# Routing the first twelve columns of a gated recurrence in one batch instead of eight and four

## The chip, the cores and the metric

The kernel runs on one core of a Trainium2 chip. A core has five engines with queues of their own: TensorE (PE in the profile, its weight loads PEld), VectorE (DVE), ScalarE (ACT), GpSimd (POOL) and SyncE (SP), which here only issues DMAs. The metric is the device time of one execution in microseconds, the median of several runs; it was 335.33 us before the change (three runs, 334.08 to 337.0).

## The reference

Two parts follow each other. The first is a gated linear recurrence over 768 steps for 4 batches and 8 heads of width 48: a complex state is multiplied by a gate of modulus at most 0.999, an outer product of k and v is added to its real part, and q reads it.

```
scale = np.minimum(mag, 0.999) / (mag + 1e-06)
new_re = ar * S_re - ai * S_im ;  new_im = ar * S_im + ai * S_re
S_re, S_im = (new_re + kv, new_im)
y[:, :, t] = np.einsum('bhd,bhde->bhe', q[:, :, t], S_re)
```

The second is a layer of eight experts over the 3072 tokens of width 384 that the first gives. Each token goes to the one expert with the largest logit, where a bias chosen by the token's modality (0 or 1) is added to the logit, and the result is scaled by the softmax weight of that expert.

```
logits = x @ w_gate + modality_bias[modality_id]
e_idx = np.argmax(logits, axis=1)
h = np.maximum(x[mask] @ w1[e], 0.0)
out[mask] = gate_w[mask, None] * (h @ w2[e])
```

## The kernel before

**Units and turns.** The 768 steps are cut into six chunks of 128, so with four batches there are 24 units of 128 tokens. A loop of turns (L450, w from -4 to 24) is a software pipeline over them. In turn w the kernel issues the transposes of unit w+2 (`turned`: PE writes tKT and tQT, ACT copies them to KT and QT), the products inside the chunk of unit w+1 (`inner`: wp, masked by DVE to W, and up, from which DVE makes mid, U and the next state), the output of unit w (`outer`: yp, copied by ACT to yT) and the token rows and logits of unit w-1 (`rows`: xw, whose rows ACT casts into a tile `packed`, and whose logits DVE sums into `lg`, L389). One unit is one column of 128 tokens for the routing.

**Gates.** Two units form a group x. Their gates go through squares, logarithms, tangents, a running sum of angles on PE (`angles`, u, L197) and one of logarithms (`sums`, ls, L243), sines (css) and moduli (pm). Even turns run the logarithm and exponential functions on ACT, odd ones arctangent and sine, each behind a table load (L117). `hats` (L264) multiplies q and k by the waves to QK (L283), which the transposes read. Squares of the last group are made in turn 13.

**Order.** A scheduler lays the instructions of each engine in a fixed queue; an engine runs its queue in order and waits at an instruction until what it needs is there. Some orders are written out by hand: `issue_after` places an instruction behind another, `mark` is such a place, and `ORDERED` (L306) puts the mask of some units behind a hat. All loads go through SP's queue: the gates' parts (L132, L133), q and k (L139, L140), v (L288), the running sums of the chunk before (cb, L207), and the eight-byte modality numbers (`mid`, L576).

**PSUM.** Every product writes a tile that `pair` or `bank` hands out from four slots in rotation (`bufs=4` in `pair`), so a product waits for the reader of the tile that was handed out four earlier.

**Routing.** `make_router` runs at the end of turn 0: constants, the loads of the modality numbers and biases (L574, L576), and from them the bias of every token and expert with five DVE instructions (L592 to L596). `takes` (L396) says when a batch of columns is routed: columns 0 to 7 in turn 8, 8 to 11 in turn 12, 12 to 15 in turn 16, 16 to 19 in turn 20, the rest in turn 24. `Router.take` is a generator that `resume` (L442) carries on. Its first part (L622 to L653) adds the bias, finds the best expert as a one-hot matrix `oneh` and adds up counts `acc`. One turn later its second part has PE count the tokens that go before each token (`rank`, L656 to L663) and DVE makes of it the slot `place` of each row in a table x_rows in DRAM. For the first batch `guess` (L772) then takes the first two experts in use, from a product `cnt` (L705). In later turns the rows are stored, two columns at a time: DVE writes the softmax weight into the rows (L684) and POOL issues an indirect DMA for each column (L685). A batch below column 16 stores from three turns after its `take` on, one pair a turn. The first batch also writes the empty block of x_rows from one row in SBUF (L622).

**Experts.** `Layers` loads the first weights of the two guessed experts into buffers that the gates leave (`w1s` over abs, L882, and `w2s` over css, L891); the second is tied behind the last row store issued by then (L892). Each tile of 256 or 128 rows is loaded (xg, L929), transposed, multiplied by w1 (h_ps, L966) and w2 (y_ps, L981), and scattered (L986). Behind each expert's last token `fill` (L690) copies empty rows from DRAM to DRAM, so that a tile that reaches past the last token reads rows that no output takes; the loads of the first four tiles don't wait for them.

Of the kernel before, what the change touches and what calls it, by code (L numbers as in the profile page):

```python
# [23 lines left out]
def gate_loop(nc, ctx, tc, cpool, ident, q, k, v, a_re, a_im, sel, lg, make_router, make_layers):  # L24
# [345 lines left out]
    def rows(g, b):  # L370
# [9 lines left out]
        m0 = max(c for c in takes.values() if c <= m)  # L380
        if m == m0:
            n = min([c for c in takes.values() if c > m] + [NU]) - m
            packed = un.tile([L, n, Router.W], U32, name=f"packed{n}", bufs=1 if n == 8 else 2)
            nc.gpsimd.iota(packed[:, 0:n, Router.W - 1].rearrange("p (g b) -> p g b", b=B), pattern=[[L, n // B], [S, B]], base=g * L, channel_multiplier=1)
            box["packed"] = packed
        packed = box["packed"]
# [9 lines left out]
    takes = {7: 0, 11: 8, EARLY - 1: 12, 19: EARLY, NU - 1: 20}  # L396
# [53 lines left out]
    for w in range(-4, NU + 1):  # L450
# [12 lines left out]
        else:  # L463
# [5 lines left out]
            if w > 3:  # L469
                hats(n + 4)  # L470
# [10 lines left out]
        unit(inner, n + 1)  # L481
        resume(lambda w0, n: n > 1 and w0 < EARLY and w >= w0 + 3)
# [19 lines left out]
        resume(lambda w0, n: n == 1 or w0 >= EARLY and w >= w0 + 2)  # L502
        if w - 1 in takes:
            open_.append([rt.take(takes[w - 1], w, late, box["packed"], lambda n: dense(box["full"][:, 0], n)), w, 1])
            next(open_[-1][0])
# [9 lines left out]
class Router:  # L515
# [20 lines left out]
    def __init__(self, nc, ctx, tc, keep, ps, bank, lg, x_rows, moe_modality_id, moe_modality_bias, N, Dt, E, B, G):  # L536
# [35 lines left out]
        mb = rc.tile([TP, nM, E], F32, name="mb")  # L572
        mid = rc.tile([TP, NT, 2], I32, name="mid")
        nc.sync.dma_start(out=mb.rearrange("p m e -> p (m e)"), in_=moe_modality_bias.rearrange("m e -> (m e)")[None, :].broadcast_to([TP, nM * E]))  # L574
        for b in range(B):
            nc.sync.dma_start(out=mid.rearrange("p (g b) w -> p b g w", b=B)[:, b], in_=moe_modality_id[b * G * TP:(b + 1) * G * TP].bitcast(I32).rearrange("(g p w) -> p g w", p=TP, w=2))  # L576
# [11 lines left out]

        bias = self.bias = rc.tile([TP, NT, E], F32, name="bias")
# [7 lines left out]
        self.acc = None  # L597
# [9 lines left out]
    def take(self, m0, m1, late, packed, dense):  # L607
# [4 lines left out]
        M = 8  # L612

        def t(name, shape, dt=F32):
            full = rp.tile([TP, M] + shape, dt, name=name)
            return full[:, 0:n]
# [60 lines left out]
        for i in range(n):  # L677
            if i % 2 == 0:
                if i:
# [3 lines left out]
                with self.tc.issue_after(self.mark.ins):  # L683
                    nc.vector.reciprocal(packed[:, i:i + 2, self.W - 2].bitcast(F32), sums[0][:, i:i + 2])  # L684
# [417 lines left out]
```

## Time and profile before

| | us |
|---|---|
| median of three runs | 335.33 |
| the profiled execution | 336.66 |
| its span, from the first to the last instruction | 335.1 |
| PE busy, 4955 matmuls | 296.6 |
| DVE busy | 243.4 |
| ACT busy | 240.5 |
| POOL busy | 65.7 |

The span is what the trace covers; the time of the execution holds 1.6 us more around it. Rows of the trace begin with the start in us from the span's begin and the duration in us; at the end, in brackets, stands how long the engine was idle before, and what ended it. A view by windows gives for each stretch its length, then the busy time of PE, PEld, DVE, ACT and POOL with the number of instructions, the clock that was granted to TensorE as a share of full speed, the share of DMA engines busy and the GB/s. The view of one source line gives for each kind of instruction the count, the shortest, median and longest duration in ns, and the first and last start. The recurrence takes about the first 250 us; the expert layers take the rest.

### The profile page before, as it was taken

How to read it: one execution, taken by the hardware profiler on the slowest of the kernel's cores; microseconds unless marked ns; L12 is line 12 of the kernel's file. 1: busy time of each engine (PE TensorE's matmuls, PEld its weight loads, DVE VectorE, ACT ScalarE, POOL GpSimd, SP SyncE). 2: the span in 40 equal slices, each digit the busy share in tenths (PEclk: the TensorE clock that was granted, in tenths of full speed). 3: DMA queues.
4: the chain of work that ended last, by engine and by line, in shares of the span. 5: the costliest groups of instructions: out<-in, count | busy, mean ns of one | idle time of the engine just before them, and what ended most of it. 6: DMA issues, size and time to landing. Idle time of an engine off the chain costs nothing.

```text
span 335.1 us, 11585 instructions
## 1 busy us (share of the span) xinstructions
PE 296.6 (89%) x4955; PEld 228.7 (68%) x4955; DVE 243.4 (73%) x464; ACT 240.5 (72%) x290; POOL 65.7 (20%) x92
## 2 busy tenths in 40 slices
PE   1685999899989999997999999999997699999991
PEld 0342576577787868684786879888895377777770
DVE  2759699999999989968599969972458433646430
ACT  3888799999998999796797978535235356454541
POOL 8000000000000000002134224034034425242423
PEclk9999799999999999997899999999999789999997
DMA  7968898799776767798379972114912722333211
GB/s 146 208 129 162 148 200 141 124 179 180 164 131 153 134 146 41 129 220 153 83 146 161 177 165 51 25 50 64 223 54 84 226 94 97 104 110 107 103 67 56
DMA packets 155282, 43.04 MB, mean 128 GB/s; under 512 B 145602, under 2 KB 151494, under 8 KB 155096
## 3 DMA queue, kind: packets, MB, share of 16 engines
q1 hardware_dynamic: 149592, 31.98, 49.9%
q0 software_dynamic: 5632, 10.25, 11.4%
q8 instruction: 41, 0.67, 0.8%
q14 instruction: 17, 0.14, 0.1%
HBM read 38.00 MB, written 9.15 MB: 141 GB/s over the span
## 4 chain that ended last, share of the span: by engine, by line
PE 47%; ACT 22%; SPq 10%; DVE 6%; DMA 5%; issue 5%; POOL 1%; another core or an unknown queue 1%; POOLq 0%; DVEq 0%; ACTq 0%
PE h_ps L966 9%; PE y_ps L981 9%; PE up L336 5%; ACT sq L120 5%; PE xw L377 4%; ACT L117 4%; ACT css L120 3%; PE yp L366 3%; ACT pm L120 3%; PE ls L243 3%; PE wp L326 3%; PE u L197 3%; DMA qk<-in_k_dram 2%; PE yp L360 2%; SPq L132 2%
## 5 line engine op out<-in xcount | busy, mean ns | idle before, releaser
L685 POOL DMA_INDIRECT x_rows<-packed,place x24 | 29.6, 1233 | 66.2 <-DVE packed L684 17.6
L283 DVE TENSOR_TENSOR QK<-css,qkp 128x1536 f32<-128x1536 f32 x24 | 42.0, 1750 | 0.2
L981 PE MATMUL y_ps<-w2t,hT 128*128 128x384 bf16 x200 | 37.3, 341 | 3.9 <-ACT hT L969 3.9
L336 PE MATMUL up<-V,QK 64*96 64x48 f32 x704 | 37.8, 247 | 1.7 <-DVE lg L389 1.6
L336 PEld LDWEIGHTS up<-V,QK 64*96 64x96 f32 x704 | 34.7, 161 | 3.8 <-DVE lg L389 2.4
L966 PE MATMUL h_ps<-xgT,w1t 128*128 128x256 bf16 (+1 forms) x312 | 35.3, 270 | 0.0
L986 POOL DMA_INDIRECT out_dram<-y_sb,xg x25 | 24.9, 996 | 43.5 <-ACT y_sb L984 39.5
L966 PEld LDWEIGHTS <-w1t 128*128 128x128 bf16 x312 | 29.8, 99 | 5.0 <-issue 0.3
L117 ACT ACT_TABLE_LOAD x25 | 32.1, 1283 | 1.4 <-PEq L1086 0.9
L308 ACT COPY KT<-tKT 96x1024 f32<-96x1024 f32 x24 | 24.1, 1006 | 10.2 <-PE tKT L307 10.1
L981 PEld LDWEIGHTS <-hT 128*128 128x128 bf16 x200 | 19.4, 101 | 17.5 <-ACT hT L969 4.5
L882 POOL DMA_DIRECT2D abs<-in_moe_w_dram x2 | 1.8, 898 | 149.3 <-ACT sq L120 149.3
L984 ACT ACTIVATE y_sb<-y_ps,xg 128x384 f32<-128x384 f32 x25 | 13.2, 578 | 23.2 <-PE y_ps L981 18.8
L326 PEld LDWEIGHTS wp<-QT,KT 96*64 96x64 f32 x768 | 24.3, 138 | 8.1 <-ACT yT L367 1.9
L367 ACT COPY yT<-yp 128x512 f32<-128x512 f32 x24 | 14.0, 584 | 21.3 <-PE yp L366 21.1
L326 PE MATMUL wp<-QT,KT 96*64 96x64 f32 x768 | 27.6, 225 | 1.6 <-ACT yT L367 1.3
L377 PE MATMUL xw<-sel,yT 64*128 64x56 f32 x384 | 27.4, 277 | 1.0 <-ACT QT L308 0.6
L197 PE MATMUL u<-tan,turn 128*128 128x384 f32 x48 | 22.4, 550 | 5.0 <-ACT yT L367 2.4
L377 PEld LDWEIGHTS xw<-sel,yT 64*128 64x128 f32 x384 | 24.1, 187 | 3.1 <-ACT QT L308 0.7
L308 ACT COPY QT<-tQT 96x1024 f32<-96x1024 f32 x24 | 24.3, 1012 | 0.3 <-PE tQT L307 0.3
L120 ACT ACTIVATE sq<-sq 128x1536 f32<-128x1536 f32 (+1 forms) x20 | 23.3, 1165 | 1.4 <-DVE sq L151 1.3
L969 ACT ACTIVATE hT<-h_ps 128x1024 bf16<-128x1024 f32 (+1 forms) x17 | 16.9, 999 | 8.9 <-PE h_ps L966 3.0
(198 smaller groups left out, 594.7 us busy)
## 6 DMA issues: line engine op xcount, KB each, us to landing
abs<-in_a_re_dram SPq DMA_DIRECT2D x24, 192.0 KB
abs<-in_a_im_dram SPq DMA_DIRECT2D x24, 192.0 KB
qk<-in_q_dram SPq DMA_DIRECT2D x24, 192.0 KB
qk<-in_k_dram SPq DMA_DIRECT2D x24, 192.0 KB
V<-in_v_dram SPq DMA_DIRECT2D x24, 192.0 KB
cb<-f_scr SPq DMA_DIRECT2D x10, 384.0 KB
xg<-x_rows SPq DMA_DIRECT2D x12, 194.0 KB
x_rows<-x_rows SPq DMA_DIRECT2D x8, 194.0 KB
```

Source lines behind the costliest of these rows:

```text
L117: then(nc.scalar.preload_act_table_set(name))
L120: then(nc.scalar.activation(*args, **kw))
L197: nc.tensor.matmul(us[:, i], turn[:], tan[:, i], start=True, stop=False)
L283: box["hat"] = nc.vector.tensor_tensor(QK[:].rearrange("p a h c d -> p a (h c d)"), wave, twice, Alu.mult)
L308: nc.scalar.copy(to[:], tp)
L326: nc.tensor.matmul(wp[rows_, h, :], KT[:, s, h], QT[:, s, h], start=True, stop=True)
L336: ins = nc.tensor.matmul(up[:, s, h], flat[rows_, h * C:(h + 1) * C], V[rows_, h, 0:D], start=True, stop=True)
L377: ins = nc.tensor.matmul(xw[:, u, j], yT[at_u, j], sel[at_u, j], start=True, stop=True)
L685: put = self.put = nc.gpsimd.indirect_dma_start(out=self.x_rows, out_offset=bass.IndirectOffsetOnAxis(ap=place[:, i:i + 1], axis=0), in_=p ...
L966: nc.tensor.matmul(h_ps[:, f // nf, f % nf, :], w1t[:, k, ff * 128:(ff + 1) * 128], xgT[:, k, :], start=(k == 0), stop=(k == KD - 1))
L981: nc.tensor.matmul(y_both[:, s], self.hT[:, f, s * 128:(s + 1) * 128], w2t[:, f, :], start=(f == 0), stop=(f == NF - 1))
L986: sc = self.sc = nc.gpsimd.indirect_dma_start(out=self.out, out_offset=bass.IndirectOffsetOnAxis(ap=xg[:, Dt // 2 + 1:], axis=0), in_=y_sb ...
```

## The change

Four edits are made.

- Columns 0 to 11 are routed as one batch in turn 12; the batch of eight in turn 8 is gone, and with it the one of four. `guess` and the write of the empty block move with it. The rows of these columns are still kept in a tile of eight and tiles of four. Their stores begin in turn 15, with columns 8 to 11, two pairs in that turn and one in each later one, up to turn 19.
- The loads of the modality numbers and biases move from turn 0 to turn 8, and the five DVE instructions from turn 0 to turn 12, behind the mask of that turn.
- In turn 15 the hat of unit 19 is issued behind the mask instead of ahead of it.
- Each fill copies 128 empty rows instead of 256.

```
-            if w > 3:
+            if w > 3 and w != 15:
                 hats(n + 4)
...
+        if w == 15:
+            with tc.issue_after(box["masked"].ins):
+                hats(n + 4)
...
-    takes = {7: 0, 11: 8, EARLY - 1: 12, 19: EARLY, NU - 1: 20}
+    takes = {11: 0, EARLY - 1: 12, 19: EARLY, NU - 1: 20}
...
+        if w == 8:
+            rt.load_bias()
+        if w == 12:
+            with tc.issue_after(box["masked"].ins):
+                rt.make_bias()
-        resume(lambda w0, n: n == 1 or w0 >= EARLY and w >= w0 + 2)
+        resume(lambda w0, n: n == 1 or w0 >= EARLY and w >= w0 + 2 or w0 < EARLY and w == w0 + 3)
...
-        M = 8
+        M = 12 if n == 12 else 4
...
-        for i in range(n):
-            if i % 2 == 0:
-                if i:
+        for k, i in enumerate(list(range(8, n)) + list(range(min(n, 8)))):
+            rows, c = packed(m0 + i)
+            if k % 2 == 0:
+                if k:
...
-            self.put_row(nc.sync.dma_start(out=self.x_rows[bass.ds(n0, 2 * self.TP), :], in_=self.blank), True)
+            self.put_row(nc.sync.dma_start(out=self.x_rows[bass.ds(n0, self.TP), :], in_=self.blank[0:self.TP]), True)
```

`load_bias` and `make_bias` hold the lines that were in the router's constructor:

```
    def load_bias(self):
...
        nc.sync.dma_start(out=mb.rearrange("p m e -> p (m e)"), in_=moe_modality_bias.rearrange("m e -> (m e)")[None, :].broadcast_to([TP, nM * E]))
        for b in range(B):
            nc.sync.dma_start(out=mid.rearrange("p (g b) w -> p b g w", b=B)[:, b], in_=moe_modality_id[b * G * TP:(b + 1) * G * TP].bitcast(I32).rearrange("(g p w) -> p g w", p=TP, w=2))
    def make_bias(self):
...
        for m in range(nM):
            is_m = rc.tile([TP, NT], F32, name="is_m")
            nc.vector.tensor_scalar(is_m[:], mid[:, :, 0], float(m), None, Alu.is_equal)
```

More of the change, by code (lines that the diff above doesn't have):

```diff
@@ L571, in __init__ @@
         nc.gpsimd.memset(self.fast[:, self.NE + self.NR:self.NE + self.NR + 1], 1.0)
[L572 to L576, printed above, removed]
         self.io = rc.tile([TP, 32], F32, name="io")
@@ L611, in take @@
         last = m1 == len(self.tile_of)
-        M = 8
+        M = 12 if n == 12 else 4
         def t(name, shape, dt=F32):
-            full = rp.tile([TP, M] + shape, dt, name=name)
+            full = rp.tile([TP, M] + shape, dt, name=name + str(M), bufs=1 if M == 12 else 2)
             return full[:, 0:n]
```

30 lines of the change are left out of this document (21 added, 9 removed).

## The prediction

> **What bounds the kernel now.** I began with the page's span and engine shares, and then cut the span into pairs of loop turns.
>
> ```profile
> span 335.1 us, 11585 instructions
> PE 296.6 (89%) x4955; PEld 228.7 (68%) x4955; DVE 243.4 (73%) x464; ACT 240.5 (72%) x290; POOL 65.7 (20%) x92
> ```
> ```profile
> core 0: us, PE busy (x) PEld busy (x) DVE busy (x) ACT busy (x) POOL busy (x), PEclk, DMA share, GB/s
> 85.77:102.63 16.86, 15.72 (x352) 12.86 (x348) 16.14 (x24) 16.36 (x19) 0.00 (x0) 1.00 0.74 144
> 137.49:157.63 20.14, 16.66 (x362) 13.87 (x363) 17.30 (x40) 16.58 (x20) 1.01 (x1) 0.91 0.89 167
> 157.63:179.39 21.76, 20.69 (x392) 15.75 (x391) 16.88 (x35) 16.54 (x19) 7.35 (x6) 0.92 0.66 123
> 195.44:211.78 16.34, 16.28 (x384) 13.85 (x385) 14.38 (x31) 11.52 (x14) 4.89 (x4) 1.00 0.42 95
> ```
>
> The shares mislead: ACT's 72% is a mean of two halves. From 85 us on, ACT has 16.4 us of work in a pair of turns whatever the pair takes, and fills a pair of 16.9. DVE is close behind. The pairs that begin at 137 and 157 are 3 to 5 us longer with no more ACT work in them, and of the pairs shown they alone have a granted clock of PE under 1.00. By 195 PE is the bound. So the question is what stops ACT between 137 and 179. ACT's timeline says it; yT is copied once per turn, and these are the odd turns 7 to 17 with the longest idle times between them:
>
> ```profile
> 118.97 0.59 ACT L367 COPY yT<-yp 128x512 f32<-128x512 f32 x1
> ...
> 135.84 0.59 ACT L367 COPY yT<-yp 128x512 f32<-128x512 f32 x1
> ...
> 138.46 1.01 ACT L308 COPY KT<-tKT 96x1024 f32<-96x1024 f32 x1 [1.65 <-PE tKT L307]
> ...
> 152.13 1.49 ACT L120 ACTIVATE sq<-abs 128x1536 f32<-128x1536 f32 x1
> ...
> 154.93 0.59 ACT L367 COPY yT<-yp 128x512 f32<-128x512 f32 x1
> ...
> 160.53 1.01 ACT L308 COPY KT<-tKT 96x1024 f32<-96x1024 f32 x1 [4.63 <-PE tKT L307]
> ...
> 177.25 0.59 ACT L367 COPY yT<-yp 128x512 f32<-128x512 f32 x1
> ...
> 194.44 0.59 ACT L367 COPY yT<-yp 128x512 f32<-128x512 f32 x1
> ...
> 210.12 0.59 ACT L367 COPY yT<-yp 128x512 f32<-128x512 f32 x1 [2.25 <-PE yp L366]
> ```
>
> The periods are 16.87 (turns 7 to 9), 19.09 (9 to 11), 22.32 (11 to 13), 17.19 (13 to 15) and 15.68 (15 to 17). I take 17.0 as undisturbed: 16.87, and 16.86 for the pair from 85.77. The excess is then **2.1 us** in turns 9 to 11 and **5.3 us** in turns 11 to 13. PE's rows give the cause:
>
> ```profile
> 135.12 0.91 PE L197 MATMUL u<-tan,turn 128*128 128x384 f32 x2
> ...
> 136.84 0.19 PE L659 MATMUL rank<-oneh,tri 128*128 128x64 bf16 x1
> 136.87 0.32 PE L663 MATMUL rank<-oneh,ones 128*128 128x56 bf16 x7
> ```
> ```profile
> 155.57 1.65 PE L197 MATMUL u<-tan,turn 128*128 128x384 f32 x2 [2.43 <-ACT yT L367]
> 161.59 0.91 PE L243 MATMUL ls<-lm,half 128*128 128x384 f32 x2 [0.58 <-ACT KT L308]
> ```
> ```profile
> 150.78:154.19 3.41, 2.36 (x69) 2.08 (x60) 3.41 (x5) 3.39 (x4) 0.25 (x1) 1.00 0.73 107
> 154.19:157.60 3.41, 2.03 (x4) 1.24 (x5) 3.41 (x5) 1.70 (x3) 0.76 (x1) 0.50 0.96 185
> 157.60:161.02 3.42, 3.41 (x35) 1.95 (x34) 2.09 (x5) 0.49 (x1) 2.05 (x2) 0.50 1.09 206
> 62.03:65.45 3.42, 2.29 (x20) 1.72 (x21) 3.42 (x6) 3.39 (x6) 0.00 (x0) 1.00 0.83 69
> ```
>
> All PSUM tiles share four rotating slots. In turn 9 the routing of the first eight columns takes two of them (rank and cnt). From then until the next routing every product reuses the slot of another reader than before: in turn 11, u (155.57) stands 2.43 us until yT is copied, where u of turn 9 follows xw at once. Then the granted clock is 0.50 for 6.8 us, and tKT reaches ACT 4.63 us late.
>
> **The change part by part.** I sum against the profiled execution (336.66 us, span 335.1) and shift the result to the median.
>
> *Turns 9 to 13: the early routing goes.* No rank and cnt in turn 9, so in the built order u of turn 11 waits for DVE as in other turns. What is late next is ACT itself. Both periods fall to 17.0: **-2.1 and -5.3**. Bounds: nothing, if something else holds u; -8.2 for both at the 16.6 us of ACT's busy time.
>
> *The biases.* Five DVE instructions move from turn 1 to turn 12, and their five loads from turn 0 to turn 8.
>
> ```profile
> L592 DVE TENSOR_SCALAR is_m<-mid x2: 164/164/165, 68.7 to 70.0; 128x24 f32<-128x24 int32 x2
> L594 DVE TENSOR_TENSOR bias<-is_m,mb x1: 349/349/349, 69.6 to 69.6; 128x192 f32<-128x192 f32 x1
> 60.50 2.41 SPq L576 DMA_DIRECT2D mid<-in_moe_modality_id_dram  x4
> ```
>
> Their durations add to 2 x 0.16 + 3 x 0.35 = 1.4 us; overlapping their neighbours they hold DVE about 1.0. Taking them from turn 1, where ACT is the bound, and SP's 2.4 us with them, I put at **-0.2** (0 to -1.4). On SP they now stand in turn 8 ahead of V and qk, whose users come two turns later: 0, up to +2.4 if that cover goes. The write of the empty block, in turn 8 so far, moves to turn 12, a like place with fewer loads: 0 (-1 to +2).
>
> *Turn 13: twelve columns routed at once.* In the built order, turn 13's DVE work is W, l, mid, mx, U, sh, state, cand, the sum of squares, best, oneh. Compare turn 9:
>
> ```profile
> 133.60 0.68 DVE L327 TENSOR_TENSOR W<-wp,mask 128x512 f32<-128x512 f32 x1
> ...
> 135.38 0.22 DVE L635 TENSOR_TENSOR oneh<-cand,best 128x64 bf16<-128x64 f32 x1
> ...
> 136.16 0.55 DVE L348 TENSOR_TENSOR state<-U,mt 96x384 f32<-96x384 f32 x1
> 136.62 0.95 DVE L151 TENSOR_TENSOR sq<-sq 128x768 f32<-128x768 f32 x1
> ```
>
> From the start of W to the end of oneh were 2.0 us there. Each overlaps the next by some 0.09, so I count W at 0.6, three like state at 0.46, the sum of squares at 0.87 and six small ones at 0.18 (an estimate for 96 elements, from 0.22 less the overlap for 64): 3.9. The biases delay W by 1.0, less 0.3 for l and mx, which stood ahead of it. So oneh is 2.6 us later than in turn 9, where it ended at 135.60, 1.24 us ahead of the first rank matmul at 136.84. PE, in order, stands **about 1.4 us** at rank (0.5 to 2.6); queued behind it are cnt, both transposes, ls and wp, and ACT's KT copy waits for them. The period 13 to 15 is then 19.09 (turns 9 to 11 with the same slots) + 1.4 + 0.2 for four more rank matmuls - 1.4 for the square of 152.13 that turn 15 no longer has = 19.3, against 17.19 now: **+2.1** (0 to +4). That the second batch of four no longer runs here is in this comparison.
>
> *Turns 15 to 17.* The shifted slots now hold here, and u of turn 15 waits for yT in the built order.
>
> ```profile
> 194.52 0.91 PE L197 MATMUL u<-tan,turn 128*128 128x384 f32 x2
> ```
>
> Without the square, yT is copied by 195.03, so u stands 0.5 us and ls perhaps 0.6 as at 161.59: **+1.1** (0 to +2.4, the hole of turn 11). The qkp and QK of unit 19, moved behind W in turn 15, feed a turn whose bound is PE: 0.
>
> *POOL and the weights.* The first twelve columns' rows now leave in turns 15 to 19, so up to two more indirect stores stand ahead of the first w2 load.
>
> ```profile
> 229.24 0.97 POOL L685 DMA_INDIRECT x_rows<-packed,place  x1 [0.30 <-issue]
> 230.20 0.95 POOL L891 DMA_DIRECT2D css<-in_moe_w_dram  x1
> 231.00:243.40 12.40, 12.40 (x300) 11.23 (x300) 5.36 (x20) 4.21 (x7) 1.22 (x3) 1.00 1.08 178
> 246.65 0.94 DVE L920 COPY w2t<-css 128x3072 bf16 x1
> ```
>
> They delay it by 2 x 1.28 = 2.6 us. Its traffic ends at 243.4 and its last user begins at 246.65, so 3.2 us cover it: 0 (to +2 where the stores take twice as long). Without that cover DVE would stand at w2t with the next lg queued behind it, and PE with it.
>
> *Empty rows.* Eight fills of 194 KB become 97 KB.
>
> ```profile
> 255.85 9.89 SPq L699 DMA_DIRECT2D x_rows<-x_rows  x8
> 267.12 0.16 DVE L806 TENSOR_SCALAR column<-smine 1x19 int32<-1x19 f32 x1
> ```
>
> The next loads on SP's queue need the columns that DVE makes at 267.12, when the fills have been issued (255.85 + 9.89 = 265.74): 0 (-3 if their traffic is what slows PE's second tile).
>
> Sum: -2.1 - 5.3 - 0.2 + 2.1 + 1.1 = **-4.4 us**. 336.66 becomes 332.3; the median of 335.33 becomes **331.0**.
>
> **A rule against the row.** The trace has the clock at 0.50 behind a gap of 2.43 us, and at 1.00 in the window from 62.03 with 1.1 us of PE idle. The Trainium skill ("TensorE: Matmul & The Clock Gate", section "HAM oscillation — how this bites in real kernels") says that only idle gaps of PE over about 3.4 us throttle it. By that rule the gap of turn 11 would have cost no clock, and removing it less; this trace disagrees, and the sum goes by the trace.
>
> **The rivals.** (B) *The stall moves whole.* PE's wait at rank in turn 13 is the mechanism. If PE idles as in the window from 150.78 (1.05 us of 3.41) with that window's light work, the clock halves there too, and u of turn 15 finds the full hole. The moved stretch then costs what the old one did, 2.1 + 5.3, less the 0.2 of excess that turns 13 to 15 have now, plus 0.7 for W and the 1.4 at rank: 336.66 - 7.6 + 9.3 = 338.4, or 337.0 by the median, slower than before. It decides from 1.05 us of idle; my 1.4 is above that, but 62.03 shows 1.1 without a drop, which is why this is not the forecast. (C) *The tail gains.* PE's second expert tile around 260 runs beside the fills; if they slow it, half the bytes give another 3 us: 328. Against it: no row shows an engine waiting for them. (D) *It does not do what it says*: u of turn 11 is held by another late copy, and only turn 9's share goes, which turn 13 returns: 335.
>
> **How the numbers follow.** Forecast 0.48, B 0.30, C 0.10, D 0.12. One per cent, 3.4 us, is about what a measurement of this kernel tells from no change. The forecast's own range is 328.5 to 333.5; two thirds of it is more than 1% faster. With C nearly whole, faster is 0.44. Slower takes a third of B, and its bounds with two late terms, the w2 load and the empty block's write: 0.18. The rest, 0.38, is within 1%. The range runs from C's lower part, 326, past B to 338.5.
>
> **What would show it.** Right: no idle of 2 us at u of turn 11, a granted clock of 1.00 through turns 11 and 12, two periods near 17; rank of turn 13 waiting for DVE oneh or acc; a period near 19 for turns 13 to 15. Wrong: a clock of 0.5 around turns 13 to 16; ACT still idle for over 1 us at KT in turn 12; idle of DVE ahead of w2t.

## The result, and the profile after

The changed kernel takes **354.78 us** (median of five runs, 349.28 to 359.86) against 334.62 us before: a ratio of 1.051, with a 95% interval of 1.037 to 1.066. Forecast were 331.0 us and a range up to 338.5. The profiled execution took 354.78 us, its span is 353.2 us. Ratios, here and below, compare only the executions near the fastest of each kernel (here 349.28 and 354.51 us, with a granted clock of 0.93 and 0.92 over the span, where the profiled execution before had 0.97), so they are not quotients of the medians.

The head of the page after, with the granted clock of PE in 40 slices of 8.8 us:

```profile
span 353.2 us, 11567 instructions
PE 316.6 (90%) x4954; PEld 246.2 (70%) x4954; DVE 243.3 (69%) x451; ACT 240.2 (68%) x289; POOL 67.0 (19%) x92
PEclk9989899999999999999999855975569899999998
```

The same line of the page before:

```profile
PEclk9999799999999999997899999999999789999997
```

DVE and ACT work as long as before (243.3 and 240.2 us); PE is busy 20 us longer with one matmul less. The early dip (7 in the 19th slice before) is gone; in its place the 23rd to 30th slices, 194 to 265 us, lie between 5 and 9. Cut into pairs of loop turns (turns 9 to 11, 11 to 13, 13 to 15, 15 to 17, then 17 to 19 and 19 to 22), the columns as in the prediction:

```profile
138.68:156.18 17.50, 17.01 (x392) 14.14 (x394) 16.14 (x23) 16.49 (x20) 0.00 (x0) 1.00 0.88 162
156.18:174.14 17.96, 16.66 (x348) 13.06 (x342) 17.85 (x34) 16.33 (x19) 0.00 (x0) 1.00 0.59 97
174.14:193.55 19.41, 17.68 (x405) 14.74 (x407) 15.82 (x39) 15.23 (x20) 1.80 (x2) 1.00 0.76 132
193.55:217.40 23.85, 22.21 (x350) 19.67 (x348) 14.26 (x33) 11.64 (x14) 11.45 (x9) 0.64 0.48 104
217.40:236.83 19.43, 18.52 (x371) 15.47 (x368) 12.11 (x45) 7.48 (x12) 9.29 (x6) 0.85 0.16 43
236.83:266.68 29.85, 29.85 (x472) 26.95 (x470) 9.40 (x27) 7.02 (x11) 3.94 (x5) 0.58 0.50 88
```

The first two rows are what was hoped for: 20.14 and 21.76 us have become 17.50 and 17.96, at a clock of 1.00. From 193.55 on the clock is 0.64, 0.85 and 0.58. The yT copies of the odd turns 9 to 17 on ACT's timeline say the same without DVE's part in it:

```profile
137.68 0.59 ACT L367 COPY yT<-yp 128x512 f32<-128x512 f32 x1
...
155.18 0.59 ACT L367 COPY yT<-yp 128x512 f32<-128x512 f32 x1
...
172.05 0.59 ACT L367 COPY yT<-yp 128x512 f32<-128x512 f32 x1
...
190.32 0.59 ACT L367 COPY yT<-yp 128x512 f32<-128x512 f32 x1
...
215.00 0.59 ACT L367 COPY yT<-yp 128x512 f32<-128x512 f32 x1 [6.51 <-PE yp L366]
```

The periods are 17.50, 16.87, 18.27 and 24.68, in place of 19.09, 22.32, 17.19 and 15.68. From these copies the whole difference of 18.1 us adds up:

| stretch | before, us | after, us | difference |
|---|---|---|---|
| start of the span to yT of turn 9 | 135.84 | 137.68 | +1.8 |
| yT of turn 9 to turn 15 | 58.60 | 52.64 | -6.0 |
| yT of turn 15 to the last yT | 53.04 | 77.33 | +24.3 |
| last yT to the end | 87.6 | 85.6 | -2.0 |

(The last yT copies are at 247.48 and 267.65. The first row is nothing of the change: its 1.8 us are there at the first yT copy, and in a later profile of the same kernel that copy is 1.3 us earlier.)

Where the 24.3 us come from is in the windows between the switches of the clock. Every drop in these traces that ends inside the span lasts a whole number of times 3.41 us (3.41, 6.83, 10.24 and so on, up to 44.4); "a window" below is one such time.

```profile
196.87:200.29 3.42, 2.44 (x53) 2.11 (x49) 0.02 (x1) 3.39 (x5) 2.22 (x3) 1.00 1.07 250
200.29:220.77 20.48, 20.48 (x302) 18.44 (x302) 14.10 (x51) 7.91 (x10) 7.21 (x5) 0.50 0.30 69
220.77:234.42 13.65, 13.12 (x311) 11.43 (x310) 9.05 (x20) 4.56 (x7) 8.69 (x6) 1.00 0.20 52
234.42:261.73 27.31, 26.92 (x363) 23.94 (x362) 5.55 (x22) 6.95 (x11) 4.53 (x6) 0.50 0.53 94
```

Half clock for 20.48 + 27.31 = 47.8 us; PE is the bound here and busy all the time, so half of it, 23.9 us, is lost. In the kernel before no drop lasted over 6.83 us. What stands ahead of the first drop, on PE's timeline in turn 16:

```profile
197.42 1.04 PE L336 MATMUL up<-V,QK 64*96 64x48 f32 x19
198.75 0.37 PE L336 MATMUL up<-V,QK 64*96 64x48 f32 x4 [0.28 <-issue]
199.46 0.40 PE L336 MATMUL up<-V,QK 64*96 64x48 f32 x5 [0.34 <-issue]
200.22 0.57 PE L336 MATMUL up<-V,QK 64*96 64x48 f32 x4 [0.35 <-issue]
```

and on POOL's at the same time:

```profile
194.54 1.09 POOL L707 DMA_INDIRECT x_rows<-packed,place  x1 [11.91 <-DMA qk<-in_q_dram]
195.93 1.21 POOL L707 DMA_INDIRECT x_rows<-packed,place  x1 [0.31 <-issue]
197.44 0.97 POOL L707 DMA_INDIRECT x_rows<-packed,place  x1 [0.30 <-issue]
198.72 0.97 POOL L707 DMA_INDIRECT x_rows<-packed,place  x1 [0.30 <-issue]
```

POOL issues the four row stores of turn 15 one right behind the other. PE, which waits for no semaphore, goes on in bursts of four or five matmuls, one burst each 0.71 to 0.76 us. PE's instructions come by DMA in blocks of 16 KB, and none of these blocks was on its way between 197.1 and 204.4, so these bursts are not a wait for one. Its signals come late as well: W on DVE, whose input wp was done at 197.5, starts at 200.27.

```profile
200.27 0.69 DVE L327 TENSOR_TENSOR W<-wp,mask 128x512 f32<-128x512 f32 x1 [3.42 <-remote]
```

The same picture, stores at 231.49, 232.76 and 234.04 and bursts up to 235.7, stands ahead of the drop at 234.42.

### The profile page after: what moved, and what is told of

Its sections match the earlier page's. It is cut to its first block, busy times and chain, and to the rows that moved or that the text cites. A ratio compares the mean times of both kernels' runs of the same rounds, so it can differ in the third digit from the quotient of the medians.

```text
span 353.2 us, 11567 instructions
## 1 busy us (share of the span) xinstructions
PE 316.6 (90%) x4954; PEld 246.2 (70%) x4954; DVE 243.3 (69%) x451; ACT 240.2 (68%) x289; POOL 67.0 (19%) x92
## 4 chain that ended last, share of the span: by engine, by line
PE 33%; issue 19%; ACT 18%; DVE 14%; POOL 6%; SPq 4%; DMA 3%; POOLq 1%; DVEq 0%; ACTq 0%
PE up L336 6%; POOL out_dram L1008 5%; PE xw L377 5%; PE yp L366 5%; ACT sq L120 4%; PE wp L326 3%; PE u L197 3%; ACT L117 3%; ACT css L120 3%; PE yp L360 3%; PE ls L243 2%; PE tKT L307 2%; PE tQT L307 2%; ACT pm L120 2%; DMA qk<-in_k_dram 2%
## 5 line engine op out<-in xcount | busy, mean ns | idle before, releaser
L336 PE MATMUL up<-V,QK 64*96 64x48 f32 x704 | 42.0, 258 | 2.5 <-DVE lg L389 1.5
L707 POOL DMA_INDIRECT x_rows<-packed,place x24 | 30.8, 1283 | 61.8 <-DVE w2t L942 24.0
L336 PEld LDWEIGHTS up<-V,QK 64*96 64x96 f32 x704 | 38.7, 172 | 5.0 <-DVE lg L389 2.2
L1003 PE MATMUL y_ps<-w2t,hT 128*128 128x384 bf16 x200 | 36.5, 336 | 1.7 <-issue 1.0
L326 PEld LDWEIGHTS wp<-QT,KT 96*64 96x64 f32 x768 | 27.4, 152 | 8.3 <-ACT yT L367 2.3
L326 PE MATMUL wp<-QT,KT 96*64 96x64 f32 x768 | 30.9, 240 | 1.7 <-ACT yT L367 1.7
L377 PE MATMUL xw<-sel,yT 64*128 64x56 f32 x384 | 30.6, 302 | 1.1 <-ACT QT L308 0.6
L377 PEld LDWEIGHTS xw<-sel,yT 64*128 64x128 f32 x384 | 26.9, 210 | 3.7 <-issue 0.9
L197 PE MATMUL u<-tan,turn 128*128 128x384 f32 x48 | 22.3, 549 | 3.1 <-ACT tan L120 2.1
L327 DVE TENSOR_TENSOR W<-wp,mask 128x512 f32<-128x512 f32 x24 | 16.4, 685 | 11.2 <-PE wp L326 7.7
```

The source lines that it names most:

```text
L197: nc.tensor.matmul(us[:, i], turn[:], tan[:, i], start=True, stop=False)
L326: nc.tensor.matmul(wp[rows_, h, :], KT[:, s, h], QT[:, s, h], start=True, stop=True)
L336: ins = nc.tensor.matmul(up[:, s, h], flat[rows_, h * C:(h + 1) * C], V[rows_, h, 0:D], start=True, stop=True)
L377: ins = nc.tensor.matmul(xw[:, u, j], yT[at_u, j], sel[at_u, j], start=True, stop=True)
L707: put = self.put = nc.gpsimd.indirect_dma_start(out=self.x_rows, out_offset=bass.IndirectOffsetOnAxis(ap=place[:, i:i + 1], axis=0), in_=r ...
L1003: nc.tensor.matmul(y_both[:, s], self.hT[:, f, s * 128:(s + 1) * 128], w2t[:, f, :], start=(f == 0), stop=(f == NF - 1))
```

## The experiments

Theories held at the start: **S**, a run of row stores on POOL holds PE up, and the clock falls for it; **L**, it is the two w1 loads in a row (180.61 and 181.84) that crowd the queues, and the stores only happen to be there; **H**, at half clock only products that fill the array bring the clock back. **E**, on the write of the empty block, was formed later. The kernel before, run beside each group, took about 337 us in some groups and about 329 us in others, so each kernel is compared with its own group alone. The chip does not tell the two kinds apart: the one numbered 7 in the record gave 329 us in two groups and 337 us in a third. What does is open.

### Stores in a row (before: 336.8 us)

One pair of stores a turn:

```
-        resume(lambda w0, n: n == 1 or w0 >= EARLY and w >= w0 + 2 or w0 < EARLY and w == w0 + 3)
+        resume(lambda w0, n: n == 1 or w0 >= EARLY and w >= w0 + 2)
```

> The changed kernel, with the rows of columns 0 to 11 stored one pair a turn (turns 15 to 20) instead of two pairs in turn 15. In the changed kernel PE issues in bursts with pauses of 0.57 us at 198.2 to 200.2 and again at 232.3 to 235.7, while POOL issues four and three indirect stores one right after the other, and the granted clock falls to 0.50 at 200.29 and 234.42. Theory S (a run of four stores holds PE up, and the clock falls for it): no pauses and a clock of 1.00 through turns 15 to 17; the stores of two batches still meet in turns 18 and 19, so the second drop may stay; 338 to 347 us. Theory L (both w1 loads in a row crowd the queues and hold PE up; the stores only happen to be there): the first drop stays, 350 to 358 us.

Measured 349.4 us, 1.040 (1.029 to 1.051). The first drop is gone, the second stays. In its profile the clock is 1.00 up to 225.04:

```profile
190.00:225.04 35.04, 32.03 (x717) 26.98 (x718) 28.72 (x78) 18.01 (x24) 17.76 (x12) 1.00 0.46 98
225.04:252.35 27.31, 26.16 (x346) 23.02 (x347) 5.62 (x22) 7.05 (x11) 7.26 (x9) 0.50 0.56 103
```

and POOL has the stores that precede it, four at 221.82, 223.10, 224.38 and 225.66:

```profile
221.82 0.98 POOL L707 DMA_INDIRECT x_rows<-packed,place  x1 [0.30 <-DVE mid L341]
...
225.66 0.98 POOL L707 DMA_INDIRECT x_rows<-packed,place  x1 [0.30 <-issue]
```

PE's bursts stand from 222.4 to 227.0. Turn 18 and turn 19 released their pairs while POOL was held by an earlier store, so they left together. This speaks for S; the median lies above what S named, since the second drop took 27.3 us.

The second w1 load moved behind the stores of turn 17:

```
-        for s in range(2):
+        for s in range(1):
             nc.gpsimd.dma_start(out=self.w1s[:, s:s + 1], in_=self.w1[:, bass.ds(self.guessed(s), 1)])
...
+        if turn == 17:
+            got = self.nc.gpsimd.dma_start(out=self.w1s[:, 1:2], in_=self.w1[:, bass.ds(self.guessed(1), 1)])
+            self.tc.add_manual_dep(got.ins, self.rt.put.ins.name, ...)
```

> The changed kernel with the second w1 load behind the stores of turn 17 instead of right behind the first at 181.8 us; the stores are as they were. Theory L (the two loads together crowd the queues, and PE's pauses at 198 come of it): no pauses in turn 15, first drop gone, 340 to 348 us. Theory S (the run of four stores): pauses and drop stay, within 1% of the changed kernel's 354.8 us, 350 to 359 us.

353.8 us (347.5 to 359.5): nothing won, as S had it. The profile is divided: no bursts behind the stores of turn 15 (197.15 to 201.45), though one pause of 1.39 us, up to 199.54, and no long drop there, as L had it; the bursts stand behind the stores of turn 17 (212.9 to 214.8), and the drop that lasted is the second, 13.65 us from 234.52, where no load of w1 is near. So the loads bear on which run of stores does harm, but L explains neither the second drop nor the time.

The kernel before, with the stores of columns 8 to 11 all in turn 15 and those of 12 to 15 all in turn 18:

```
-        resume(lambda w0, n: n == 1 or w0 >= EARLY and w >= w0 + 2)
+        resume(lambda w0, n: n == 1 or w0 >= EARLY and w >= w0 + 2 or w0 == 12 and w == 15)
+        resume(lambda w0, n: w0 == 16 and n > 1 and w == 18)
```

> The kernel before, with the two pairs of stores of columns 8 to 11 both in turn 15 and those of columns 12 to 15 both in turn 18; nothing else is changed. Theory S: PE pauses behind these stores and the clock falls in or after turn 15 or 18, where few full-array products follow; 339 to 350 us. Theory L: 332 to 337 us, as the kernel before, and a clock of 1.00 there.

351.6 us (343.4 to 367.7) against 336.8, a little over what S named. Its profile has a drop of 13.65 us from 235.11, right behind four stores (229.56 to 234.14). It also has one of 10.24 us from 98.58, ahead of any row store: PE was busy for 2.47 us of the window before that, with waits of 0.42 us for yT and 0.72 us for lg. The yT copies of turns 5 and 6 are 14.28 us apart there, 9.58 before, so 4.7 us of this profile's loss are not the stores'. The kernel before with the write of the empty block in turn 5 (further down) has the same two waits at the same times, but its windows begin 0.66 us later and hold 2.99 and 2.69 us of busy PE, and there the clock stays at 1.00. Where the windows happen to begin may have a part in what one execution shows.

The same kernel in another group, with the changed kernel itself, before at 337.8:

> The kernel before with the stores of columns 8 to 11 all in turn 15 and those of 12 to 15 all in turn 18, again. Theory S: slower than the kernel before by 7 us and more where PE pauses behind four stores, and within 1% of it where it doesn't.

> The changed kernel itself, beside the others. In the last three runs no PE pauses stand behind a run of four stores, and the kernel before was at 329.4 us in place of 336.8 (another chip). Theory S: the loss hangs on these pauses. Where they show in the trace, 348 to 360 us with the clock at 0.50 for 40 us behind turn 15; where they don't, the clock stays at 1.00 there and the change is 1 to 5 us faster than the kernel before of the same call, as the sum of the prediction had it (-4.4). If the loss came back without pauses, S would fall.

The kernel with the burst: 361.3 us (355.3 to 364.0). The changed kernel: 351.5 us, 1.035 (1.028 to 1.042), with drops of 17.06 us from 201.49 and 27.30 from 232.21. So two lines that only put stores together turn the kernel before into one as slow as the changed one. In the profile of the second run, which has no drop at 98 us, four stores leave between 224.40 and 228.98, PE's bursts stand from 227.1 to 230.7, and then:

```profile
223.27:230.09 6.82, 5.65 (x115) 4.82 (x111) 3.04 (x7) 0.70 (x1) 4.77 (x5) 1.00 0.14 46
230.09:274.47 44.38, 43.96 (x565) 39.27 (x565) 12.69 (x41) 10.73 (x19) 5.88 (x7) 0.50 0.36 66
```

The DMA share of 0.14 in the first row says that full queues aren't needed for it. The four stores of turn 15 in these two runs left no long drop behind them.

Six memsets of 128x256 on POOL between one pair and the next, for columns 0 to 15:

```
+                if k % 2:
...
+                    for _ in range(6):
+                        self.space = nc.gpsimd.memset(self.scratch[:], 0.0)
...
```

> The changed kernel with six small POOL memsets (2 to 2.5 us) between one pair of stores and the next for columns 0 to 15; the turns in which the pairs are released are as in the changed kernel, two pairs in turn 15 among them. Theory S in its narrow form (it is the stores one right behind the other, not their number in a turn): no bursts of PE 0.57 us apart, no long drop, within 2% of the kernel before (331 to 343 us where that is 337). Rival (the number of stores in these turns, or the bytes): pauses and drops as in the changed kernel, 347 to 358 us.

345.5 us, 1.026 (1.013 to 1.038), before at 337.5. Neither side: the first long drop is gone, but with pairs 3.6 us apart PE still shows two or three pauses behind a pair (from 228.5 and from 232.9 on, up to 0.38 us each), and the clock falls at 236.08 for 13.65 us. So stores need not be four in a row to go with pauses.

### What brings the clock back

Four full-array products ahead of the transposes of units 18, 20 and 22 (before at 336.8):

```
-    FILLED = {2: 10, 3: 5, 4: 5, 5: 5, 15: 4}
+    FILLED = {2: 10, 3: 5, 4: 5, 5: 5, 15: 4, 18: 4, 20: 4, 22: 4}
```

> The changed kernel with four full-array bf16 products of 512 columns (warm 0.22 us, at half clock 0.43 us each) ahead of the transposes of units 18, 20 and 22 (turns 16, 18 and 20). In the changed kernel the clock stays at 0.50 for 20.5 and 27.3 us although PE is 100% busy in those windows with products of 64 or 96 rows, and returns behind windows that hold full-array products (ls at 217, rank at 258). Theory H (at half clock only full-array products bring the clock back): each fill ends a drop within two windows of 3.4 us; half clock after 190 us is about 15 us in place of 48, worth some 16 us less 2.6 us for the fills: 338 to 345 us. Rival (the clock returns when the cause of the stall is over): half clock as long as before, 354 to 360 us.

342.4 us, 1.019 (1.009 to 1.030): in the range. But not the way it was expected. The first drop, at 201.09, ended after 6.83 us with no fill in it. The fill of unit 22 stood at 230.01, among the pauses, and no second drop came:

```profile
227.91:231.33 3.42, 3.10 (x35) 1.98 (x31) 0.00 (x0) 0.00 (x0) 2.56 (x3) 1.00 0.23 77
```

The same fills on a quarter of the array (64 rows and 64 columns), before at 337.8:

```
+                for _ in range(4 if u in (18, 20, 22) else 0):
+                    nc.tensor.matmul(full[0:64]..., halfb[0:64, 0:64], halfb[0:64, None, :].broadcast_to([64, 4, L]), start=True, stop=True)
```

> The changed kernel with the fills on 64 rows and 64 columns, again, since without pauses there was no drop that they could end. Where pauses and a drop show: theory H has the clock stay at 0.50 for 20 us and more, 350 to 360 us; the rival (busy time counts) 338 to 346 us. Where none show: 1% at most from the kernel before.

353.8 us (345.5 to 368.3). The fill of unit 22 stands at 234.32, and the drop comes and stays:

```profile
231.43:234.84 3.41, 2.75 (x39) 2.11 (x34) 0.00 (x0) 0.00 (x0) 2.80 (x3) 1.00 0.28 92
234.84:262.15 27.31, 27.31 (x365) 23.94 (x364) 5.56 (x22) 7.05 (x11) 3.97 (x6) 0.50 0.52 92
```

PE is busy in all 27.31 us, at half clock. Counted over the 20 profiles of this case, between 60 and 300 us there are 146 windows at half clock: of the 69 without a 128x128 product 5 were the last of their drop, of the 58 in which such products took 1.5 us or more of PE's time 48 were. Those five are the fullest of the 69, if fullness is the sum of rows x columns x streamed columns over the products that start in a window. That fits H in a softer form, the used share of the array counts; this is a count after the fact, and what exactly is measured, the runs don't say.

An earlier run of the same kernel fell into a group with before at 329.4:

> The changed kernel with fills at the same places and of the same length as those that brought it to 342 us (four bf16 products of 512 columns ahead of the transposes of units 18, 20 and 22), but on 64 rows and 64 columns of the array in place of 128 and 128. Theory H (what counts for the clock is the part of the array that works): the clock stays at 0.50 for 20 us and more behind turn 15 or 18, as without fills; 352 to 360 us. Rival (what counts is PE's busy time, or that a product is long): the clock returns as with the full fills; 338 to 346 us.

327.9 us, 0.999 (0.995 to 1.003). Here four stores in a row, from 195.22 to 200.95, had no effect at all:

```profile
195.22 1.09 POOL L709 DMA_INDIRECT x_rows<-packed,place  x1 [11.91 <-DMA qk<-in_q_dram]
...
199.41 1.54 POOL L709 DMA_INDIRECT x_rows<-packed,place  x1 [0.31 <-issue]
```
```profile
195.15:201.97 6.82, 6.82 (x156) 5.51 (x154) 5.77 (x9) 6.44 (x8) 4.81 (x4) 1.00 0.95 199
```

PE has no pause and no drop up to the end of the recurrence. So S holds in the groups where the kernel before takes 337 us, and not in those where it takes 329. The changed kernel itself was not run in one of the latter; this kernel is the changed one with three fills of 1.05 us, and its median stands 1.5 us under the kernel before, which the interval does not tell from none. Without the 3.15 us of fills it might stand 3 to 5 us under, near the forecast gain; that is an estimate, and no run shows it. The kernel before itself differs between the two kinds of groups by 1.4 us up to the last yT copy (247.48 against 246.04, in the profile of the small edits below) and by 6.8 us behind it, where the slower one has a drop of 6.83 us from 263.42 and the other none.

### The small edits

The kernel before with fills of 128 rows and the hat of unit 19 behind the mask, nothing else (before at 329.4):

> The kernel before with the two small edits alone: fills of 128 empty rows in place of 256, and the hat of unit 19 behind the mask in turn 15. The prediction priced both at 0; every theory held here puts the loss on the stores: 332 to 340 us, the same as the kernel before. If one of these edits costs by itself (the queue of DVE or PE in turn 15, or the rows behind an expert's last token): over 341 us.

329.3 us, 0.9995 (0.996 to 1.004). Both cost nothing.

One pair of stores a turn from the end of turn 14 on, columns 12 to 15 in turns 19 and 20, full fills at units 20 and 22; first with before at 329.4, then at 337.8:

> The changed kernel with at most two stores in a row up to turn 18 (columns 0 to 11 one pair a turn from the end of turn 14 to turn 19, columns 12 to 15 in turns 19 and 20), and four full-array bf16 products of 512 columns ahead of the transposes of units 20 and 22. Theory S and H together: no drop of the clock through turn 18, where the changed kernel with one pair a turn was 4 us ahead of the kernel before; a run of four in turn 19 may still drop it for 7 us, and the fills cost 1.7 us: 329 to 336 us, the kernel before or a little under. If the drops have another cause that neither removes: 342 us and more.

> One pair of stores a turn, with full fills at units 20 and 22, again. Where pauses show behind four stores in a row: 330 to 338 us, at or under the kernel before, since the one run of four that is left (turn 19) meets a fill. Where none show: 329 to 334 us, up to 1% over the kernel before, as measured.

331.6 us, 1.011 (1.007 to 1.015), and 341.7 us, 1.012 (1.003 to 1.020). The profiled execution of the first, 327.4 us, had a clock of 1.00 from 68 us to the tail. It is the fastest of the six; the others had a lower mean clock (0.978 to 0.985 against 0.988), and no trace shows where. So what makes the median 2.2 us longer than the kernel before is not shown; two fills of 1.0 us are a part. In the second three drops of 3.41 us stand between 163 and 215 us.

### The write of the empty block

In six profiles of the changed kernel and its variants PE stands in yp of turn 12 for 0.94 to 1.78 us, here in the second profile of the changed kernel:

```profile
162.51 0.65 PE L366 MATMUL yp<-QT,mid 96*48 96x64 f32 x15 [0.95 <-issue]
```

The write of the empty block (256 rows, all read from one partition) ran in turn 12 up to 160 us, in packets of 776 bytes that took 370 ns each, and PE's next block of instructions (16 KB, one DMA packet) started to load behind it, at 160.18, where it started at 159.76 in the first profile, which has no such pause. Three more profiles with the write in turn 12 have none either, nor have the four of the kernel before and its variants with the write in turn 8. So the write was put back into turn 8 (before at 337.5):

```
         self.mb, self.mid = mb, mid
+        nc.sync.dma_start(out=self.blank[None], in_=self.empty[:, None, :].broadcast_to([1, 2 * TP, self.W]))
```

> The changed kernel with the write of the empty block in turn 8, as before the change, in place of turn 12. In four of the runs PE pauses for 1.2 to 2.0 us at the same instruction in turn 12, when a block of PE's instructions (16 KB) starts to load 0.2 to 0.7 us later than in the changed kernel's first trace, right behind that write. If the write delays that block: no pause there, 0 to 3 us less than the changed kernel; the drops behind the stores stay: 345 to 356 us. If it doesn't: the pause stays.

355.2 us, 1.057 (1.040 to 1.074). The pause moved with the write, to 139.7 us (1.32 us), right behind it. What nobody had expected is that the hole of turn 11 came back:

```profile
158.06 0.91 PE L197 MATMUL u<-tan,turn 128*128 128x384 f32 x2 [2.43 <-ACT yT L367]
```

rank and cnt stand in turn 13 here, so they aren't its cause. u reads nothing of yT; only the PSUM slot that it was given can make it wait for that copy. With all remedies together, the write in turn 8 among them, the hole was there too:

> All remedies together: one pair of stores a turn with the memsets between pairs, the write of the empty block in turn 8, full-array fills at units 20 and 22. Theories S and H and the one on the empty block: no pauses up to turn 20, clock 1.00 from turn 5 to turn 20, 328 to 336 us where the kernel before is 337. If pauses of another origin remain: at 340 us or over, as without the memsets.

347.8 us, 1.032 (1.022 to 1.043). Theory **E**: it is the write in turn 8 that changes the order in which PSUM tiles are handed out, so that u three turns later waits for yT. It was moved alone, in the kernel before (before at 328.6):

```
-        if m0 == 0:
-            nc.sync.dma_start(out=self.blank[None], in_=self.empty[:, None, :].broadcast_to([1, 2 * TP, self.W]))
...
+        if w == 20:
+            rt.nc.sync.dma_start(out=rt.blank[None], in_=rt.empty[:, None, :].broadcast_to([1, 2 * rt.TP, rt.W]))
```

> The kernel before with one thing moved: the write of the empty block in turn 20 in place of turn 8 (routing in two batches, stores, biases and fills as they were). With the changed kernel's write put back into turn 8 the hole of turn 11 came back (u waits 2.43 us for yT, clock 0.50 behind it), although rank and cnt of the first batch stood in turn 13. Theory E (the write in turn 8 turns the order in which PSUM tiles are handed out, and u three turns later waits for ACT): no hole, clock 1.00 in turns 11 and 12, the two pairs of turns near 17 us; 329 to 333 us where the kernel before is 337, that is 4 to 8 us less. The prediction's theory (rank and cnt in turn 9 shift the slots): the hole stays and the time with it, 335 to 339 us.

331.3 us, 1.001 (0.997 to 1.006): the time of neither theory, but the trace decides. The hole is gone, and not because the group is one of 329 us: the kernel before with the small edits, in such a group too, has it. The first row is from there, the second is the same product here, which starts ahead of the copy of yT (155.18), though PE's and ACT's rows come in the same order in both:

```profile
156.25 1.65 PE L197 MATMUL u<-tan,turn 128*128 128x384 f32 x2 [2.43 <-ACT yT L367]
```
```profile
153.65 0.91 PE L197 MATMUL u<-tan,turn 128*128 128x384 f32 x2
```

Turns 9 to 11 keep their 19.10 us, with the routing still in turn 9, and turns 11 to 13 take 16.90 in place of 22.3, at a clock of 1.00:

```profile
136.10:155.20 19.10, 17.59 (x377) 14.33 (x376) 18.97 (x43) 16.59 (x21) 1.00 (x1) 1.00 0.87 180
155.20:172.10 16.90, 16.50 (x367) 13.37 (x366) 15.82 (x31) 16.46 (x20) 10.03 (x6) 1.00 0.79 130
```

By the 22nd yT copy, of turn 21, the kernel is 7.7 us ahead of the kernel before's profile (230.8 against 238.5), which is from a group of the other kind, and 6.3 us ahead of the small edits' (237.0). Then this execution, which took 333.4 us, loses that again, in turn 22, where PE waits for its instructions behind the write (issued at 226.14):

```profile
237.21 0.69 PE L326 MATMUL wp<-QT,KT 96*64 96x64 f32 x6 [3.49 <-issue]
```
```profile
x_rows<-empty SPq DMA_DIRECT2D x1, 194.0 KB, 9.4
```

(9.4 us from issue to landing; the block of instructions started at 234.98.) The clock falls at 236.27 for 20.48 us. The fastest executions of this kernel took 327.1 us at a mean clock of 0.98 and 0.99; they can hardly have had that drop in full, and where they lost the lead no trace shows. The same with the write in turn 5, and the changed kernel (one pair a turn, fills) with the write in turn 20:

> The kernel before with the write of the empty block in turn 5. Theory E: no hole in turn 11; but in turns 5 to 7 ACT is the bound and the queues are half full, so loads behind the write may come late by up to 3 us, and a block of PE's instructions with them: 330 to 337 us where the kernel before is 337. The prediction's theory: hole and 335 to 341 us.

> The changed kernel with one pair of stores a turn, the full fills at units 20 and 22, and the write of the empty block in turn 20. Theories S, H and E: neither the pause of turn 12 nor u waiting for ACT in turn 15; 331 to 338 us where the kernel before is 337. If one batch of twelve costs more than that (the wait at rank in turn 13, the stores that meet in turn 19): 339 to 346 us.

334.6 us, 1.021 (1.016 to 1.026): no hole in turn 11, but turns 9 to 11 took 24.0 us. Its trace shows another order on DVE: W of turn 9, whose wp started at 133.03, stands behind the QK of two hats and starts at 142.20; PE stands 2.57 us at cnt until it is done, and the clock is 0.50 for one window from 143.62. So the write's place moves the built order too, not only the slots. And 336.7 us, 1.024 (1.018 to 1.029): a pause of 2.99 us at 240.8 and a drop of 20.48 us, as in the kernel before with that write.

Last, the write made short: the empty row on 128 partitions, in turn 18, with the old write taken out as above (before at 328.9).

```
-        empty = rc.tile([1, self.W], U32, name="empty")
+        empty = rc.tile([TP, self.W], U32, name="empty")
...
+        if w == 18:
+            rt.nc.sync.dma_start(out=rt.blank.rearrange("(a p) w -> p a w", p=rt.TP), in_=rt.empty[:, None, :].broadcast_to([rt.TP, 2, rt.W]))
```

> The kernel before, with the empty rows made on 128 partitions and written in turn 18 as 16 rows per DMA engine, in place of 256 rows read from one partition in turn 8. With the write in turn 20 from one partition the kernel before was 7.7 us ahead at the yT copy of turn 22 (230.8 against 238.5), and then lost it: PE stood 3.76 us for a block of its instructions behind the write's packets (365 ns each), and the clock fell for 20.5 us. Theory: it is the long packets that keep the block away, and the write's place in turn 8 that makes u wait in turn 11. Then neither hole nor pause, clock 1.00 from turn 5 to the tail, and 5 to 8 us less than the kernel before of the same call. If any write there keeps the block away: pause and drop as in turn 20, within 1% of the kernel before.

**323.3 us, 0.984 (0.979 to 0.988)**, 1.6% under the kernel before; the changed kernel was not run in this group. Its packets take 39 ns each in place of 365. The write was issued at 203.13, a block of PE's instructions started at 203.89, and PE did not stand. There is no hole either, and turns 11 to 13 are as short as expected:

```profile
156.50:173.40 16.90, 16.50 (x367) 13.32 (x366) 15.79 (x32) 16.47 (x20) 10.08 (x6) 1.00 0.82 131
```
```profile
PEclk9979799999999999999999999999999999999998
```

The last yT copy is at 241.14, 4.9 us ahead of the small edits' profile. This kernel routes in eight and four, as before the change. Two things differ from the write in turn 20, the place and the 128 partitions; a write out of one partition in turn 18 was not run, so the share of each is not shown.

## Why the prediction was wrong, point by point

**Turns 9 to 11, -2.1.** Measured 19.09 to 17.50, -1.6. The step was right, and its cause too: in the kernel before with the write in turn 20 the routing stays in turn 9 and the hole is gone, and this pair keeps its 19.1.

**Turns 11 to 13, -5.3.** Measured 22.32 to 16.87, -5.45. The size was right, the cause wrong. The prediction put the hole on the two slots that rank and cnt take. The write of the empty block in turn 8 made it: with that write in turn 8 the hole is there without rank and cnt, and without it the hole is gone with them. The prediction priced the moved write at 0; it is in fact the edit from which most of the gain comes. That a wait of 2.43 us and the half clock behind it were worth this much was read rightly; that the edit would remove them was luck.

**The biases, -0.2.** The stretch from the first yT copy to that of turn 9 took 81.91 us before and 81.92 us after, so nothing was won; the loads in turn 8 cost nothing there either.

**Turn 13, +2.1.** PE waited 1.17 us at rank (1.4 expected), the pair took 18.27 (19.3 expected), which is +1.1. Right, and a little milder:

```profile
174.37 0.20 PE L680 MATMUL rank<-oneh,tri 128*128 128x96 bf16 x1 [1.17 <-DVE lg L389]
...
190.96 0.91 PE L197 MATMUL u<-tan,turn 128*128 128x384 f32 x2 [1.06 <-ACT yT L367]
...
194.53 0.91 PE L243 MATMUL ls<-lm,half 128*128 128x384 f32 x2 [0.66 <-ACT KT L308]
```

**Turns 15 to 17, +1.1.** u stood 1.06 us and ls 0.66, against 0.5 and 0.6: the waits came where they were told, that of u twice as long. Yet the pair took 24.68 us, +9.0 in place of +1.1, and the clock stayed at 1.00 through these waits; the rest of it is the next point.

**POOL and the weights, 0 (to +2): the step that failed.** It saw that the first twelve columns' rows leave later, and priced the stores as time on POOL's queue ahead of the w2 load. That part held: no copy of w2t waited for a load. What it put at nothing, without a reason, is PE: two pairs in one turn are four stores in a row, and in groups like this one PE stands in bursts while they run. The trace of before had single pauses of this kind behind pairs of stores (0.21 us with PE idle ahead of 225.62, for one), and the prediction passed over them. With them came the second omission: it knew drops of 6.83 us alone, in turns with u and ls. In turns 16 to 22, where most products use 64 or 96 rows, the two drops lasted 20.48 and 27.31 us, 23.9 us of loss in all. How a store reaches PE stays open, and so does why some groups of runs show nothing of it.

**Empty rows and the hat, 0.** 0.9995 together: right. Rival C, a gain of the tail by smaller fills, is out with it.

**The rivals.** B named the clock, and the sign. But it put the halving at rank in turn 13 and u in turn 15, where the clock stayed at 1.00, and so missed place and size: 337.0 against 354.8. In the chances, two thirds of 0.48 and the whole of C make 0.42 for faster, not 0.44.

**The rule against the row.** The prediction weighed that idle gaps of PE of over 3.4 us throttle it, and went by the trace. That was right: the longest gap ahead of the drop at 200.29 was 0.35 us. The Trainium skill ("TensorE: Matmul & The Clock Gate", section "A second HAM failure mode: psum-queue depth-cycling") tells of clocks that oscillate where PE micro-idles between groups of matmuls. That is a second way, which the prediction's "only" leaves out. This trace agrees in part: the clock fell behind bursts with gaps of 0.28 to 0.35 us, but it did not swing back, it stayed at 0.50 for 20.48 us. The same page (section "What's actually happening") has the full clock return after one busy window. Here six and eight windows in a row were busy to 100% and 99% at 0.50, so this trace disagrees.

## What to carry to other kernels

When rows or results are stored later, look at how many stores then stand together, not only at what queues behind them, and at what PE does meanwhile; in these runs a short pause of PE was dear where no product that fills the array followed soon. A hole in a schedule that is laid out by a program may hang on an edit that has nothing to do with the engine that waits: before the gain is credited to one edit of several, move each alone. A write of many rows out of one partition is worth trying over all 128, and at another place: here the two together brought 1.6%.

## What the runs showed of the hardware

- Row stores by indirect DMA on POOL hold PE in some groups of runs: bursts of four to five matmuls each 0.71 to 0.76 us, and signals up to 3.4 us late (200.27). In other groups, with the kernel before at 329 in place of 337 us, the same four stores did nothing. What passes between the stores and PE, and why it depends on the group, stayed open; smaller stores were not tried.
- The granted clock fell after a window of 3.41 us with 2.44 us of PE busy and no gap over 0.35 us (196.87 to 200.29). Stretches at 0.50 lasted up to 44.4 us though PE was busy for 99% of it. Busy time alone does not decide: the window of the kernel before from 62.03, with 2.29 us, had no drop behind it, and one with 2.75 us had (231.43, with the 64x64 fills).
- PE's instructions come in 16 KB packets through the same DMA engines (41 packets, 0.67 MB in the page of the kernel before). Behind 256 rows of 776 bytes from one partition (365 ns a packet, 9.4 us in all) such a packet came late enough in some profiles to stop PE, for 0.72 us in turn 6, 0.94 to 1.78 us in turns 10 and 12, and 2.99 and 3.49 us in turn 22, each behind the write; in eight others, with the write in turn 8 or 12, it did not. Spread over 128 partitions and in turn 18 (39 ns a packet) it did not either.
